# Where the operands of the MLP matmuls begin in SBUF: moving ones at a multiple of 64 bytes, stationary ones 32 past it

## The chip, the cores and the metric

The kernel runs on one core of one Trainium2 chip. The metric is device time of one execution in microseconds; three runs of the kernel before gave 1395.46, 1397.22 and 1397.25, median 1397.22.

## What is computed

Attention over 4 batches, 12 heads, 448 positions and 64 values a head, with the scores mixed across heads before the softmax and the weights mixed across heads after it. Its output, 1792 tokens of 768 values, goes through two MLPs one after the other; only the MLPs are touched here.

```python
def _moe_ref(x, w_in, w_out):              # first MLP
    h = x @ w_in                           # 1792x768 @ 768x2048
    g = np.where(h > 0.0, h, np.exp(np.minimum(h, 0.0)) - 1.0)
    return (g @ w_out).astype(np.float32)  # 1792x2048 @ 2048x768

def _moe2_ref(x, w_in, w_out):             # second MLP
    h = x @ w_in
    r = np.maximum(h, 0.0)
    return ((r * r) @ w_out).astype(np.float32)

x = np.ascontiguousarray(attn_out.transpose(0, 2, 1, 3)).reshape(B * S, H * D)
x = _moe_ref(x=x, **moe_kwargs)
return _moe2_ref(x=x, **moe2_kwargs)
```

## The kernel before

The attention runs first, and loads of the first weights and of x begin in its last steps. Then `Mlps.run` takes the 1792 tokens in two halves of 896. A half passes four stages: m = 0 is the first MLP, with its in-layer (x to h) and its out-layer (h to a new x), m = 1 the second, with its in-layer (x to h) and its out-layer (h to the output). Eight stages in all.

Every float32 operand is kept as two float32r tiles, a high part and the rest (`xh` and `xl`, `hh` and `hl`, `wh` and `wl`), and a product is three matmuls, written by `three` (L576 to L578): high by high, high by low, low by high, into one PSUM bank. A matmul streams its moving operand past a stationary one, which a weight load (PEld in the profile) put there while the matmul before it ran; here every matmul has a weight load of its own.

- In-layers (`inner`): stationary is a 128x128 block of a weight tile, moving are 448 columns of x. 16 blocks of h by 6 blocks of the contraction by 2 token blocks by 3 parts are 576 matmuls.
- Out-layer of the first MLP (in `run`): stationary is a block of a weight tile, moving are 448 columns of h. 6 by 16 by 2 by 3 are again 576.
- Out-layer of the second MLP: the roles are exchanged, so that the output comes with tokens on partitions. Stationary are 128 columns of h, moving are 384 columns of a weight tile. 2 by 16 by 7 by 3 are 672.

The order of the instructions is written out by hand in the loops, and each engine takes its own in that order. Weights are loaded by SyncE's queue, brought to float32 and split by ScalarE and VectorE (`Weights`, `part` last); `advance` keeps each of these steps a fixed number of units ahead of the matmuls. x and h are written by ScalarE (high part) and VectorE (rest).

Where an operand begins in its partition follows from where its tile was put and from the offset in it. All offsets inside x, h and the weights are multiples of 64 bytes (448 columns are 1792 bytes, 128 columns 512), so the start of the tile decides alone. In the kernel before, `xh`, `xl` and all buffers of `wh` and `wl` begin 32 bytes past a multiple of 64; `hh` and `hl` begin at a multiple of 64.

Of the kernel before, what the change touches and what calls it, by code (L numbers as in the profile page):

```python
# [8 lines left out]
F32R = mybir.dt.float32r  # L9
# [6 lines left out]
B, H, S, D = 4, 12, 448, 64  # L16
# [4 lines left out]
JC, NJ = 4, 112  # L21
KC, FC = DM // 128, DFF // 128
WU = 512
EXP_MIN, EXP_MAX = 2.0**-15, float.fromhex("0x1.dffffep+16")


# [367 lines left out]
class Weights:  # L394
# [6 lines left out]
    def __init__(self, nc, dram, layers):  # L401
        self.nc = nc
        self.units = []
        kept = [dram.tile([count, 128, n], F32, name=f"{name}f", tag=f"{name}f") for name, _, count, n in layers]
        for half in range(2):
            for k, (name, src, count, n) in zip(kept, layers):
                self.units += [(half, src[i], k[i], n) for i in range(count)]
        self.raw, self.single, self.parts, self.keep = {}, {}, {}, []
        self.loaded = self.sized = self.turned = self.done = self.used = 0

    def load(self, room=None):
        i = self.loaded
        self.loaded += 1
        half, src, kept, n = self.units[i]
        if half == 0:
            self.raw[i] = (room() if room else self.pool.tile([128, WU, 2], I32, name="wd", bufs=4))[:, :n, :]
            self.nc.sync.dma_start(out=self.raw[i].rearrange("p n t -> p (n t)"), in_=src.bitcast(I32))
        else:
            self.single[i] = self.pool.tile([128, WU], F32, name="wf", bufs=6)[:, :n]
            self.nc.sync.dma_start(out=self.single[i], in_=kept)  # L420

    def size(self, room=None):

        i = self.sized
        self.sized += 1
        half, src, kept, n = self.units[i]
        if half == 1:
            return
        f = (room() if room else self.pool.tile([128, WU], F32, name="wf", bufs=6))[:, :n]
        self.nc.scalar.activation(f, self.raw[i][:, :, 1].bitcast(F32), AF.Abs)  # L430
        self.single[i] = f
# [5 lines left out]
    def turn_op(self, k):  # L437

        nc = self.nc
        i = self.turned  # L440
        half, src, kept, n = self.units[i]
        if half == 0:
            if self.sized == i:
                self.size()
            t, f = self.raw[i], self.single[i]
            low, high, w = t[:, :, 0], t[:, :, 1], f.bitcast(I32)
            if k == 0:
                nc.vector.tensor_scalar(f, f, EXP_MIN, EXP_MAX, ALU.max, ALU.min)
            elif k == 1:
                nc.vector.tensor_scalar(w, w, 5, 2, ALU.logical_shift_left, ALU.logical_shift_right)  # L450
            elif k == 2:
                nc.vector.scalar_tensor_tensor(w, high, -0x40000000, w, ALU.bitwise_and, ALU.bitwise_or)
            else:
                nc.vector.scalar_tensor_tensor(w, low, 29, w, ALU.logical_shift_right, ALU.bitwise_or)  # L454
                del self.raw[i]
                self.keep.append((kept, f))
        self.turned += k == 3

    def part(self, engine=None):
        nc = self.nc  # L460
        i = self.done
        self.done += 1
        f = self.single.pop(i)
        n = self.units[i][3]
        hi = self.pool.tile([128, WU], F32R, name="wh", bufs=4)[:, :n]
        lo = self.pool.tile([128, WU], F32R, name="wl", bufs=4)[:, :n]
        nc.scalar.copy(hi, f)  # L467
        (engine or nc.vector).tensor_tensor(lo, f, hi.bitcast(F32), ALU.subtract)  # L468
        self.parts[i] = hi, lo
# [27 lines left out]
def col(i):  # L497
    return slice(i * 128, (i + 1) * 128)


class Mlps:
# [14 lines left out]
    def tmp(self):  # L516
        return self.tp.tile([128, S], F32, name="tmp", bufs=5)

    def two_parts(self, shape, pool, name):
        return [pool.tile(shape, F32R, name=f"{name}{a}", tag=f"{name}{a}") for a in "hl"]  # L520


    def plan(self, put, M, last, work, early, early_ctx, score_ctx):
# [29 lines left out]

    def new_x(self, half):
        self.half, self.xraw = half, {}
        self.nx = self.two_parts([128, KC, 2 * S], self.xp, "x")

    def piece(self, i):

# [37 lines left out]
    def run(self):  # L597
        nc, weights, blocks = self.nc, self.weights, self.blocks
        self.hp = self.pool("hp", "left")
        for half in range(2):  # L600
            xh, xl = self.nx
            for m in range(2):
                hh, hl = self.two_parts([128, FC, 2 * S], self.hp, "h")
                pending = []

                def activate(p, f, bl, m=m, hh=hh, hl=hl):
                    u = g = self.tmp()
                    if m == 0:
                        nc.scalar.activation(u, p, AF.Relu, scale=-1.0)
                        nc.scalar.activation(u, u, AF.Exp, scale=-1.0)  # L610
                        nc.vector.scalar_tensor_tensor(g, u, -1.0, p, ALU.add, ALU.max)
                    else:
                        nc.scalar.activation(u, p, AF.Relu)  # L613
                        nc.vector.tensor_tensor(g, u, u, ALU.mult)  # L614

                    def rest():
                        nc.scalar.copy(hh[:, f, bl], g)
                        nc.vector.tensor_tensor(hl[:, f, bl], g, hh[:, f, bl].bitcast(F32), ALU.subtract)

                    pending.append(rest)  # L620

                def flush():
                    for rest in pending:
                        rest()
                    pending.clear()

                for f in range(FC):
                    if half == m == f == 0:
                        p = self.begun
                    else:  # L630
                        p = self.inner(xh, xl, flush)
                    for j, bl in enumerate(blocks):
                        activate(p[j], f, bl)
                flush()
                if m == 0:
                    xh, xl = self.two_parts([128, KC, 2 * S], self.xp, "x")
                    for o in range(KC):
                        p = [self.bank()[:, :S] for _ in blocks]
                        for f4 in range(4):
                            wh, wl = weights.next()  # L640
                            for j, bl in enumerate(blocks):
                                for i in range(4):
                                    f = 4 * f4 + i
                                    self.three(p[j], wh[:, col(i)], wl[:, col(i)], hh[:, f, bl], hl[:, f, bl],
                                               f == 0, f == FC - 1)
                        for j, bl in enumerate(blocks):
                            nc.scalar.copy(xh[:, o, bl], p[j])
                            nc.vector.tensor_tensor(xl[:, o, bl], p[j], xh[:, o, bl].bitcast(F32), ALU.subtract)
                    continue
                n2 = DM // 2  # L650
                for nh in range(2):
                    p = [self.bank()[:, :n2] for _ in range(7)]
                    for f in range(FC):
                        if half == 0 and nh == 0:
                            if f == 0:
                                self.new_x(1)
                            if f < 12:
                                self.load_x(f)
                            if 2 <= f < 14:
                                self.split_x(f - 2)  # L660
                        wh, wl = weights.next()
                        for i in range(7):
                            self.three(p[i], hh[:, f, col(i)], hl[:, f, col(i)], wh[:, :n2], wl[:, :n2],
                                       f == 0, f == FC - 1)
                    for i in range(7):
                        o = self.tmp()[:, :n2]
                        if i % 2:
                            nc.scalar.copy(o, p[i])
                        else:
                            nc.vector.tensor_copy(o, p[i])  # L670
                        r = half * 2 * S + i * 128
                        nc.sync.dma_start(out=self.out[r : r + 128, nh * n2 : (nh + 1) * n2], in_=o)
# [49 lines left out]
```

## Time and profile before

| | before |
|---|---|
| three runs, median | 1397.22 us |
| the profiled execution, its own time | 1395.56 us |
| its span | 1393.8 us |
| TensorE matmuls busy | 1381.4 us, 99% |
| weight loads busy | 1249.7 us, 90% |
| VectorE, ScalarE, GpSimd busy | 62%, 48%, 19% |
| granted TensorE clock | 1.00 of 2.4 GHz |

Busy time of matmuls is no measure of how densely they follow each other: each is shown with 0.34 to 0.37 us, and the next begins 0.18 to 0.21 us after it. So the step from the start of one matmul to the start of the next is what to read, in the timeline, or as the length of a stage over its number of matmuls.

### The profile page before, as it was taken

Reading aid. Unit: us, or ns where it says so; the run is one execution under the profiler, and the core shown is the slowest. Engines: PE = TensorE matmul, PEld = TensorE weight load, DVE = VectorE, ACT = ScalarE, POOL = GpSimd, SP = SyncE. Lnnn points to the kernel's source line nnn. Section 1 sums busy time; section 2 is a strip of 40 time slices with the busy share of each in tenths; the row PEclk is TensorE's granted clock in tenths of the full one; section 3 lists DMA queues with packets and bytes.
Section 4 is the critical chain, followed back from the end, with each engine's and each line's share of the span. In section 5 each row is a group of like instructions: output and inputs, shape, how many; then the busy total and the mean of one; then the engine's idle time right before and its main releaser. Section 6 shows DMA issues by size and latency. Waiting matters only on the chain.

```text
span 1393.8 us, 24193 instructions
## 1 busy us (share of the span) xinstructions
PE 1381.4 (99%) x8906; PEld 1249.7 (90%) x8906; DVE 859.0 (62%) x1928; ACT 669.6 (48%) x1504; POOL 263.4 (19%) x245
## 2 busy tenths in 40 slices
PE   7999999999999999999999999999999999999999
PEld 4888888888889999999999999999999999999998
DVE  6877778777886989766688886534442114443121
ACT  5776767676775666322354543245541113333111
POOL 3755665665554000000000000000000000000000
PEclk9999999999999999999999999999999999999999
DMA  5624633734544555544455575431221111111131
GB/s 157 198 105 146 192 106 131 205 107 130 192 137 158 180 159 177 189 148 144 143 163 154 166 253 186 150 100 54 61 68 53 46 46 46 57 56 57 36 108 40
DMA packets 104810, 174.40 MB, mean 125 GB/s; under 512 B 22675, under 2 KB 82163, under 8 KB 104691
## 3 DMA queue, kind: packets, MB, share of 16 engines
q1 hardware_dynamic: 104691, 172.85, 39.4%
q8 instruction: 70, 1.15, 0.3%
q14 instruction: 49, 0.40, 0.1%
HBM read 97.93 MB, written 36.18 MB: 96 GB/s over the span
## 4 chain that ended last, share of the span: by engine, by line
PE 98%; DVE 1%; ACT 0%; DMA 0%; issue 0%; POOL 0%; SPq 0%; DVEq 0%
PE ps_post L220 12%; PE ps_qk L576 11%; PE ps_qk L577 11%; PE ps_qk L578 11%; PE ps_mix L577 6%; PE ps_post L577 6%; PE ps_mix L576 6%; PE ps_post L576 6%; PE ps_post L578 6%; PE ps_mix L578 6%; PE ps_qk L245 6%; PE ps_qk L162 4%; PE ps_mix L191 3%; PE ps_mix L190 2%; PE ps_mix L189 2%; DMA k_room<-kr 0%
## 5 line engine op out<-in xcount | busy, mean ns | idle before, releaser
L467 ACT CAST wh<-wf 128x384 fp32r<-128x384 f32 (+1 forms) x240 | 126.6, 532 | 272.4 <-DVE wf L454 113.8
L468 DVE TENSOR_TENSOR wl<-wf,wh 128x384 fp32r<-128x384 f32 (+1 forms) x238 | 137.3, 581 | 163.2 <-ACT wh L467 162.3
L183 POOL TENSOR_TENSOR gl<-graw,gh 120x448 fp32r<-120x448 f32 x178 | 201.5, 1154 | 145.7 <-ACT gh L178 142.4
L220 PEld LDWEIGHTS ps_post<-wg,ex 120*112 120x112 f32 x1440 | 156.1, 177 | 21.6 <-DVE tot L204 7.5
L220 PE MATMUL ps_post<-wg,ex 120*112 120x120 f32 x1440 | 172.9, 272 | 0.7 <-DVE at L227 0.6
L198 ACT ACTIVATE ex<-ps_mix,nmax 120x448 f32<-120x448 f32 x180 | 113.5, 637 | 113.5 <-DVE nmax L196 110.2
L576 PE MATMUL ps_qk<-xh,wh 128*128 128x448 f32 x384 | 141.4, 368 | 0.0
L577 PE MATMUL ps_qk<-xl,wh 128*128 128x448 f32 x384 | 141.3, 368 | 0.0
L578 PE MATMUL ps_qk<-xh,wl 128*128 128x448 f32 x384 | 141.3, 368 | 0.0
L196 DVE TENSOR_REDUCE nmax<-ps_mix 120x1 f32<-120x448 f32 x180 | 109.6, 622 | 41.7 <-PE ps_mix L191 41.3
L227 DVE COPY at<-ps_post 112x480 f32<-112x480 f32 x162 | 105.4, 650 | 9.9 <-PE ps_post L220 9.9
L178 ACT CAST gh<-graw 120x448 fp32r<-120x448 f32 x180 | 95.2, 593 | 0.1
L614 DVE TENSOR_TENSOR tmp<-tmp 128x448 f32<-128x448 f32 x64 | 39.9, 623 | 77.6 <-ACT tmp L613 77.6
L165 ACT COPY sc<-ps_qk 120x448 f32<-120x448 f32 x178 | 82.2, 558 | 7.1 <-PE ps_qk L162 7.0
L245 PEld LDWEIGHTS ps_qk<-at,v 112*64 112x64 f32 x1536 | 73.8, 137 | 11.3 <-ACT gh L178 6.5
L245 PE MATMUL ps_qk<-at,v 112*64 112x110 f32 (+2 forms) x1536 | 81.8, 262 | 0.0
L576 PEld LDWEIGHTS ps_qk<-xh,wh 128*128 128x128 f32 x384 | 72.1, 188 | 7.3
L577 PEld LDWEIGHTS ps_qk<-xl,wh 128*128 128x128 f32 x384 | 72.1, 188 | 7.3
L578 PEld LDWEIGHTS ps_qk<-xh,wl 128*128 128x128 f32 x384 | 72.1, 188 | 7.2
L430 ACT ACTIVATE wf<-wd 128x384 f32<-128x384 f32 (+1 forms) x120 | 69.4, 578 | 18.0 <-DMA wd<-w2o 8.6
L577 PE MATMUL ps_qk<-wl,hh 128*128 128x384 f32 x224 | 75.9, 339 | 0.0
L576 PE MATMUL ps_qk<-wh,hh 128*128 128x384 f32 x224 | 75.8, 339 | 0.0
(137 smaller groups left out, 3155.4 us busy)
## 6 DMA issues: line engine op xcount, KB each, us to landing
graw<-sc SPq DMA_DIRECT2D x180, 210.0 KB
wd<-w1i SPq DMA_DIRECT2D x32, 384.0 KB
wd<-w1o SPq DMA_DIRECT2D x24, 512.0 KB
wd<-w2i SPq DMA_DIRECT2D x32, 384.0 KB
wd<-w2o SPq DMA_DIRECT2D x32, 384.0 KB
w1if<-wf SPq DMA_DIRECT2D x32, 192.0 KB
w1of<-wf SPq DMA_DIRECT2D x24, 256.0 KB
w2if<-wf SPq DMA_DIRECT2D x32, 192.0 KB
```

Source lines behind the costliest of these rows:

```text
L178: nc.scalar.copy(hi, graw[t])
L183: engine.tensor_tensor(lo, graw.pop(t), parts[t][0].bitcast(F32), ALU.subtract)
L196: nc.vector.tensor_reduce(nmax, p, AX.X, ALU.max, negate=True)
L198: nc.scalar.activation(e[-1], p, AF.Exp, bias=nmax, scale=1.0, accum_out=tot[:, t % 2 : t % 2 + 1])
L220: nc.tensor.matmul(p[:, c, :], e[:, c * NJ : (c + 1) * NJ], w, start=True, stop=True)
L227: nc.vector.tensor_copy(o, p)
L245: nc.tensor.matmul(p[64 * a : 64 * a + 64, k, :w], vt[b, i][:, jc, g * D : (g + 1) * D], at[n][:, jc, 6 * i + g, :w], start=(jc == 0), sto ...
L467: nc.scalar.copy(hi, f)
L468: (engine or nc.vector).tensor_tensor(lo, f, hi.bitcast(F32), ALU.subtract)
L576: mm(p, wh, xh, start=first, stop=False)
L577: mm(p, wh, xl, start=False, stop=False)
L578: mm(p, wl, xh, start=False, stop=last)
```

## The change

A constant `OFF` of 8 elements, 32 bytes, is added. Tiles of x and h are made 64 bytes longer, and the operand begins in them `at` elements in: 8 for x, 0 for the h of the first MLP, 8 for the h of the second. The weight tiles keep their size; of the second out-layer's weights (`w2o`) the parts begin 8 elements into theirs, all others at 0. The tiles themselves also move a little, because x is longer: x by 128 bytes, the weight tiles by 128 bytes, `hl` by 64. With that the operands begin, in bytes past a multiple of 64:

| stage (of each half) | matmuls | moving, stationary before | moving, stationary after |
|---|---|---|---|
| first in-layer | 576 of 448 columns | x 32, w 32 | x 0, w 32 |
| first out-layer | 576 of 448 columns | h 0, w 32 | h 0, w 32 |
| second in-layer | 576 of 448 columns | x 32, w 32 | x 0, w 32 |
| second out-layer | 672 of 384 columns | w 32, h 0 | w 0, h 32 |

No engine gets an instruction more or less, and their order is the same on each. One load of x at the end of the attention no longer waits for TensorE, since the place that its tile has now was given up earlier.

```diff
+OFF = 8
@@ class Weights
-                self.units += [(half, src[i], k[i], n) for i in range(count)]
+                self.units += [(half, src[i], k[i], n, name == "w2o") for i in range(count)]
...
-        hi = self.pool.tile([128, WU], F32R, name="wh", bufs=4)[:, :n]
-        lo = self.pool.tile([128, WU], F32R, name="wl", bufs=4)[:, :n]
+        at = OFF * self.units[i][4]
+        hi = self.pool.tile([128, WU], F32R, name="wh", bufs=4)[:, at : at + n]
+        lo = self.pool.tile([128, WU], F32R, name="wl", bufs=4)[:, at : at + n]
@@ class Mlps
-    def two_parts(self, shape, pool, name):
-        return [pool.tile(shape, F32R, name=f"{name}{a}", tag=f"{name}{a}") for a in "hl"]
+    def two_parts(self, k, pool, name, at):
+        n = k * 2 * S
+        t = [pool.tile([128, n + 2 * OFF], F32R, name=f"{name}{a}", tag=f"{name}{a}") for a in "hl"]
+        return [x[:, at : at + n].rearrange("p (k s) -> p k s", k=k) for x in t]
...
-        self.nx = self.two_parts([128, KC, 2 * S], self.xp, "x")
+        self.nx = self.two_parts(KC, self.xp, "x", OFF)
...
-                hh, hl = self.two_parts([128, FC, 2 * S], self.hp, "h")
+                hh, hl = self.two_parts(FC, self.hp, "h", m * OFF)
...
-                    xh, xl = self.two_parts([128, KC, 2 * S], self.xp, "x")
+                    xh, xl = self.two_parts(KC, self.xp, "x", OFF)
```

## Rows read from the trace of the kernel before

**Rows 1.** The page: the span, busy time by engine, TensorE's granted clock, the chain.

```profile
span 1393.8 us, 24193 instructions
PE 1381.4 (99%) x8906; PEld 1249.7 (90%) x8906; DVE 859.0 (62%) x1928; ACT 669.6 (48%) x1504; POOL 263.4 (19%) x245
...
PEclk9999999999999999999999999999999999999999
...
PE 98%; DVE 1%; ACT 0%; DMA 0%; issue 0%; POOL 0%; SPq 0%; DVEq 0%
```

**Rows 2.** The windows of the eight stages: length, TensorE busy (matmuls touched), clock.

```profile
433.82:557.59 123.77, 123.77 (x675) 1.00 0.55 175
557.59:676.63 119.04, 119.04 (x578) 1.00 0.49 160
676.63:795.65 119.02, 119.02 (x577) 1.00 0.50 157
795.65:914.38 118.73, 118.73 (x674) 1.00 0.57 184
914.38:1033.41 119.03, 119.03 (x578) 1.00 0.24 72
1033.41:1152.44 119.03, 119.03 (x577) 1.00 0.17 49
1152.44:1271.47 119.03, 119.03 (x577) 1.00 0.19 54
1271.47:1393.80 122.33, 118.88 (x673) 1.00 0.20 62
```

**Rows 3.** Timeline of TensorE, first in-layer of half 1: start us, duration us.

```profile
999.72 0.37 PE L578 MATMUL ps_post<-xh,wl 128*128 128x448 f32 x1
999.93 0.37 PE L576 MATMUL ps_mix<-xh,wh 128*128 128x448 f32 x1
1000.14 0.37 PE L577 MATMUL ps_mix<-xl,wh 128*128 128x448 f32 x1
```

**Rows 4.** Timeline of TensorE in the first out-layer of half 0.

```profile
599.75 0.37 PE L576 MATMUL ps_post<-hh,wh 128*128 128x448 f32 x1
599.95 0.37 PE L577 MATMUL ps_post<-hl,wh 128*128 128x448 f32 x1
```

**Rows 5.** Timeline of TensorE in the second out-layer of half 0.

```profile
849.71 0.34 PE L576 MATMUL ps_mix<-wh,hh 128*128 128x384 f32 x1
849.89 0.34 PE L577 MATMUL ps_mix<-wl,hh 128*128 128x384 f32 x1
850.06 0.34 PE L578 MATMUL ps_mix<-wh,hl 128*128 128x384 f32 x1
850.24 0.34 PE L576 MATMUL ps_post<-wh,hh 128*128 128x384 f32 x1
```

**Rows 6.** Timeline of TensorE: the second and the 35th matmul of the first in-layer, and what follows.

```profile
434.11 0.36 PE L577 MATMUL ps_mix<-xl,wh 128*128 128x448 f32 x1
...
440.80 0.36 PE L577 MATMUL ps_post<-xl,wh 128*128 128x448 f32 x1
...
441.30 2.81 PE L245 MATMUL ps_qk<-at,v 112*64 112x108 f32 x56
```

**Rows 7.** Window between those two starts: length, busy, matmuls touched.

```profile
434.11:440.80 6.69, 6.69 (x35) 1.00 0.24 71
```

**Rows 8.** Timeline of TensorE in the attention: matmuls of 448 columns.

```profile
109.65 0.36 PE L189 MATMUL ps_mix<-gh,pre_l 120*120 120x448 f32 x1
109.85 0.36 PE L190 MATMUL ps_mix<-gh,pre_h 120*120 120x448 f32 x1
110.05 0.37 PE L191 MATMUL ps_mix<-gl,pre_h 120*120 120x448 f32 x1
```

**Rows 9.** The groups: weight loads of 128 and of 120 columns, mean ns.

```profile
L576 PEld LDWEIGHTS ps_qk<-xh,wh 128*128 128x128 f32 x384 | 72.1, 188 | 7.3
L190 PEld LDWEIGHTS ps_mix<-gh,pre_h 120*120 120x120 f32 x180 | 32.9, 183 | 1.8
```

More of the change, by code (lines that the diff above doesn't have):

```diff
@@ L413, in load @@
         self.loaded += 1
-        half, src, kept, n = self.units[i]
+        half, src, kept, n, moves = self.units[i]
         if half == 0:
@@ L425, in size @@
         self.sized += 1
-        half, src, kept, n = self.units[i]
+        half, src, kept, n, moves = self.units[i]
         if half == 1:
@@ L440, in turn_op @@
         i = self.turned
-        half, src, kept, n = self.units[i]
+        half, src, kept, n, moves = self.units[i]
         if half == 0:
```

## The prediction

> **What bounds the kernel now.** I read the page first: TensorE is busy for 99% of the span, 98% of the chain that ended last lies on it, and its clock was granted in full, 2.4 GHz, in every slice [rows 1]. So the kernel ends when TensorE has worked off its list, and no other engine's time matters unless it makes TensorE wait. Busy time does not say how dense the list is, so I read the stages next. The window of a stage goes from the start of its first matmul to the start of the next stage's first; the counts beside the windows are one or two above the stage's own, for the matmuls that straddle an end [rows 2]. A stage of 576 matmuls of 448 columns takes 119.03 us, which is 206.7 ns from start to start: both out-layers of the first MLP, the second in-layer of either half and the first in-layer of the second half, all alike within 0.02 us. The very first in-layer takes 123.77 us for as many, since the attention's last matmuls lie within it. The second out-layer, 672 matmuls of 384 columns, takes 118.73 us, 176.7 ns each; its second run, with the end of the program behind it in its window, has 118.88 us of busy time. Inside a stage the starts follow each other evenly, 0.20 to 0.21 us apart in an in-layer [rows 3] and in a first out-layer [rows 4], 0.17 to 0.18 in a second out-layer [rows 5], and no row of them names anything waited for.
>
> At 2.4 GHz, 448 clocks are 186.7 ns and 384 are 160.0. If a column takes a clock, a matmul carries 20.0 ns on top of its columns in the in-layers and the first out-layers, and 16.7 ns in the second out-layers. Those extras are all that a change of addresses could reach: 3456 x 20.0 + 1344 x 16.7 = 69 + 22 = 91 us, of 1395.56 us for the profiled execution (1393.8 span, 1.76 around it).
>
> **The change, part by part.** Nothing is added, removed or moved on any engine's list; SyncE's, GpSimd's and the other queues are as they were. One load of x loses a wait on TensorE at the end of the attention, where TensorE is the engine that others wait for: 0. ScalarE, VectorE and GpSimd write x, h and the last weights 32 bytes further on; they are busy 48%, 62% and 19% [rows 1] and TensorE waits for none of them in these stages, so even some per cent more on their writes stays under the matmuls: 0. What is left is how TensorE reads its two operands, stage by stage.
>
> First out-layers, 1152 matmuls: moving 0 and stationary 32 before and after. The tiles shift by multiples of 64 bytes. I take 0.
>
> In-layers, 2304 matmuls: from moving 32, stationary 32 to moving 0, stationary 32. The trace has this very case: it is the first out-layer, the same 448 columns against the same weight tiles, and it takes 119.04 and 119.03 us where the in-layers beside it take 119.02 and 119.03 [rows 2]. Moving 0 with stationary 32 and moving 32 with stationary 32 cost the same 206.7 ns. By that row the change here is 0, within 576 x 4 x 0.02 ns, under 0.1 us. It is the nearest row there can be, and I take it.
>
> But the spacing is not fixed by the addresses alone. The first 36 matmuls of the first in-layer use the same x and weight tiles as the rest of that stage, and from the second to the 35th the starts go from 434.11 to 440.80 [rows 6], 33 steps in 6.69 us [rows 7]: 202.7 ns, 4.0 less than later at the same alignment. So there are at least two steady rhythms at 32 and 32. In the attention, matmuls of 448 columns follow each other after 200 ns [rows 8], with loads of 120 columns in place of 128, 183 ns in place of 188 [rows 9]. That gives the in-layers' bounds: downward 2304 x 4.0 = 9.2 us by the first rhythm, 2304 x 6.7 = 15.4 us by the attention's; upward nothing shows more than 206.7 in a steady stretch, so 0.
>
> Second out-layers, 1344 matmuls: from moving 32, stationary 0 to moving 0, stationary 32, with 384 columns. No row has 384 columns in this arrangement. Two rows are near. The same stage with the alignments exchanged has 16.7 ns over its columns; the first out-layer, with the new alignments but 448 columns, has 20.0. If the columns' number or the mere chain of load and matmul sets the extra, it stays at 176.7 ns: 0. If the alignment sets it, it becomes 160.0 + 20.0 = 180.0: 1344 x 3.3 = 4.5 us more. Downward, the attention's rows leave 13.3 ns over the columns, 3.4 less than now: 4.5 us off. I take 0, because the in-layers and first out-layers show that 32 bytes in the start of the moving operand make no difference there, and the first 36 matmuls show that the extra differs where no alignment does. The sum is 0 + 0 + 0.
>
> The Trainium skill has a rule that speaks against the change (TensorE: Matmul & The Clock Gate, section Step-by-step: what each phase is for): TensorE reads the moving operand and the weights by two independent SBUF ports, and loading the next weights takes no read bandwidth from the running matmul. By it the sum is 0 as well. Its formula for isolated matmuls (section Back-to-back issue gap) would however give 448 / 2.4 + 2.5 = 189.2 ns, an estimate that the stages' 206.7 does not bear out; something costs 17.5 ns a matmul that the page does not name, so its rule is not proof that the two reads never meet.
>
> **The rivals.** *The exchange costs the second out-layers their shorter step.* Mechanism: the weight load and the running matmul meet in SBUF, and how often is set by where each begins. For it: all steady stretches with the stationary operand at 32 have 20.0 ns over the columns, all with it at 0 have 16.7 [rows 2]. Against it: 384 columns and stationary 0 always come together in this trace, and the first 36 matmuls have 16.0 with stationary 32. It decides if the extra belongs to the alignment; then 1397.2 + 4.5 = 1401.7 us, slower by 0.32%.
>
> *The in-layers fall into the shorter rhythm.* The stretch of 202.7 ns ended when the attention's matmuls cut in after the 36th [rows 6], and from then on all stages held 206.7. A new alignment could keep the shorter one: 2304 x 4.0 = 9.2 us, 1388.0 us; with the first out-layers too 3456 x 4.0 = 13.8, 1383.4; with the attention's 200 ns in the in-layers alone 15.4, 1381.8. For it: two rhythms exist at one alignment, so small things choose between them. Against it: the first out-layers have had the new alignment all along, and were at 206.7 in both halves.
>
> *The two reads stop meeting and the extra goes nearly whole.* The sum by rows is bounded by the 46 us that 20.0 ns on 2304 in-layer matmuls are, 1351 us. The first out-layers speak against it plainly, since they would have had it before. The page's 189.2 ns would make it 2304 x 17.5 = 40 us, 1357 us.
>
> That the change does not do what it says I leave at 0: the starts of the tiles after it are at the places that it names.
>
> **How the numbers follow.** Cases: all stages as they are 0.36 (1397.2 us); second out-layers slower 0.27 (1401.7); in-layers in a shorter rhythm 0.27 (1382 to 1393, the upper end with the second out-layers slower at the same time); second out-layers shorter alone 0.05 (1392.7); the extra gone 0.04; slower by something that no row shows 0.01. A measurement of this kernel can tell about 0.2%, 2.8 us, from no change: the three runs lie 1.8 us apart. Faster by more: 0.27 + 0.05 + 0.04 = 0.36. Within: 0.36. Slower: 0.27 + 0.01 = 0.28. The likeliest is no change, 1397.2 us; its own range is 1394.5 to 1400. Since both signs hold most of the chance together, the range for 8 in 10 goes from 1382, the attention's rhythm in the in-layers, to 1403, the slower second out-layers with a microsecond of the runs' spread; beyond it lie about 0.06.
>
> **What would show it.** Right: windows of 119.0 us for each stage of 576 and 118.7 for the second out-layers, TensorE's starts still 206.7 and 176.7 ns apart. The first rival shows as 121.0 us for each second out-layer with all else equal; the second as in-layers at 116.8 us or less (and first out-layers at 119.0 or at 116.8); the third as in-layers near 109. Wrong altogether I would be if the first out-layers moved much, since their alignments are the same before and after, or if a stage's starts became uneven, with a wait named between them.

## The result, and the profile after

The changed kernel takes 1381.26 us (median of 4 runs, 1381.01 to 1382.14) against 1396.43 us of the kernel before: a ratio of 0.9893, 95% interval 0.988 to 0.9905. That is 15.2 us, 1.1%, faster, where I had forecast no change; it lies 0.7 us below the range that I gave. Of 20 executions of the kernel before, 18 took 1395.4 to 1398.0 us and two, of which there is no profile, 1380.77 and 1378.98; both of these stand beside e11 below, and its interval is wide for that.

The page of the changed kernel, its span, busy times and TensorE's granted clock, to be set beside [rows 1]:

```profile
span 1379.2 us, 24193 instructions
PE 1368.4 (99%) x8906; PEld 1248.4 (91%) x8906; DVE 859.2 (62%) x1928; ACT 669.5 (49%) x1504; POOL 263.3 (19%) x245
...
PEclk9999999999999999999999999999999999999999
```

The same instructions, the other engines' busy times unchanged to some tenths of a us, TensorE's shorter by 13 us. The windows of its eight stages, in the order and with the columns of [rows 2] (stretch, length, TensorE busy, matmuls touched, clock):

```profile
434.94:556.94 122.00, 122.00 (x675) 1.00 0.55 177
556.94:674.06 117.12, 117.12 (x577) 1.00 0.50 164
674.06:791.18 117.12, 117.12 (x577) 1.00 0.50 159
791.18:907.68 116.50, 116.50 (x673) 1.00 0.59 188
907.68:1024.80 117.12, 117.12 (x577) 1.00 0.24 73
1024.80:1141.92 117.12, 117.12 (x577) 1.00 0.17 50
1141.92:1259.04 117.12, 117.12 (x577) 1.00 0.19 55
1259.04:1379.20 120.16, 116.66 (x673) 1.00 0.19 63
```

Every stage is shorter. A stage of 576 went from 119.03 to 117.12 us, 206.7 to 203.3 ns from start to start; a second out-layer from 118.73 to 116.50, 176.7 to 173.4 ns. The differences against [rows 2], in order, are 1.77, 1.92, 1.90, 2.23, 1.91, 1.91, 1.91 and 2.22 us: 15.8 together. The MLPs begin 1.1 us later in this execution, in a stretch of mean granted clock 0.99 where the execution before had 1.00; so the spans differ by 14.6 us.

The row to stop at is the second. It is the first out-layer, whose operands begin at 0 and at 32 past a multiple of 64 before and after. By the rule in the change's name nothing happened to it, and it gained as much as the in-layers. The starts in the second in-layer of half 0 (start us, duration us), to be set beside [rows 3]:

```profile
699.68 0.36 PE L581 MATMUL ps_qk<-xh,wh 128*128 128x448 f32 x1
699.89 0.37 PE L582 MATMUL ps_qk<-xl,wh 128*128 128x448 f32 x1
700.09 0.37 PE L583 MATMUL ps_qk<-xh,wl 128*128 128x448 f32 x1
700.29 0.36 PE L581 MATMUL ps_qk<-xh,wh 128*128 128x448 f32 x1
```

Hundredths of a us hide how even the steps are. By the starts in the trace, in ns, the steps here repeat 205, 200, 205, 205, 202, 204, each to within 1 ns or 2, where those of [rows 3] are all 206 or 207.

### The profile page after: what moved, and what is told of

Same layout as the page of the kernel before. It is cut to its first block, busy times and chain, and to the rows that moved or that the text cites. A ratio compares the mean times of both kernels' runs of the same rounds, so it can differ in the third digit from the quotient of the medians.

```text
span 1379.2 us, 24193 instructions
## 1 busy us (share of the span) xinstructions
PE 1368.4 (99%) x8906; PEld 1248.4 (91%) x8906; DVE 859.2 (62%) x1928; ACT 669.5 (49%) x1504; POOL 263.3 (19%) x245
## 4 chain that ended last, share of the span: by engine, by line
PE 97%; DVE 1%; ACT 0%; issue 0%; DMA 0%; POOL 0%; SPq 0%; ACTq 0%; DVEq 0%; POOLq 0%
PE ps_post L221 12%; PE ps_qk L582 11%; PE ps_qk L583 11%; PE ps_qk L581 11%; PE ps_qk L246 6%; PE ps_mix L582 6%; PE ps_post L582 6%; PE ps_post L583 6%; PE ps_mix L583 6%; PE ps_mix L581 6%; PE ps_post L581 6%; PE ps_qk L163 4%; PE ps_mix L192 3%; PE ps_mix L190 3%; PE ps_mix L191 3%
```

## The experiments

What the change did besides its rule: the tiles of x and h became 64 bytes longer, so that `xl` and `hl` now begin 64 bytes further on, modulo 128, than `xh` and `hh`; and the weight tiles moved by 128 bytes. So I put every operand's place in its own hands. In the kernel used for most runs, tiles of x and h are 256 bytes longer than before, which leaves all of them where they were modulo 256, and a table gives each operand's start modulo 256, by stage and half:

```diff
+PAD = 64
+PLACES = {'x1': (224, 224), 'x2': (224, 224), 'h1': (128, 128), 'h2': (128, 128),
+          'w1i': (224, 224), 'w1o': (224, 224), 'w2i': (224, 224), 'w2o': (224, 224)}
+BASE = {"x": 224, "h": 128, "w": 224}
+
+def at(kind, half, part):
+    name = kind[0]
+    place = PLACES.get((kind, half), PLACES[kind])[part]
+    return (place - BASE[name]) % 256 // 4
...
+        t = [pool.tile([128, n + PAD], F32R, name=f"{name}{a}", tag=f"{name}{a}") for a in "hl"]
+        o = [at(kind, half, a) for a in range(2)]
+        return [x[:, a : a + n].rearrange("p (k s) -> p k s", k=k) for x, a in zip(t, o)]
```

The table shown is the kernel before; with these places alone the longer tiles were not run, but stages at old places or old differences are among the runs below (e4, e6, e7). A pair is the high and the low part; x1, x2, h1, h2 are x and h of the first and second MLP, w1i to w2o the four weights. The changed kernel is x 128 and 192, h1 128 and 192, h2 160 and 224, all weights 96, but w2o 128.

### Same places modulo 64, both parts together (e1_together, e8_together_again)

```diff
-PLACES = {'x1': (224, 224), 'x2': (224, 224), 'h1': (128, 128), 'h2': (128, 128),
-          'w1i': (224, 224), 'w1o': (224, 224), 'w2i': (224, 224), 'w2o': (224, 224)}
+PLACES = {'x1': (128, 128), 'x2': (128, 128), 'h1': (128, 128), 'h2': (160, 160),
+          'w1i': (96, 96), 'w1o': (224, 224), 'w2i': (96, 96), 'w2o': (128, 128)}
```

> The changed kernel shortened every stage, the first out-layers too, whose operands begin at 0 and 32 past a multiple of 64 before and after; what changed there is that hl now begins 64 bytes past hh, counted by 128. This run keeps the change's places modulo 64 in all stages (in-layers and second out-layers moving 0, stationary 32) but puts the low part of x and of h at the same place modulo 128 as the high part. Theory of 64 bytes: what counts is the start modulo 64; in-layers 117.1 us and second out-layers 116.5 us as in the changed kernel, about 1384 us in all (first out-layers as before, 119.0). Theory of the parts apart: what counts is that the two moving parts begin 64 bytes apart, so that consecutive matmuls do not start at the same place of 128 bytes; in-layers and first out-layers 119.0 us again, second out-layers unknown, about 1393 to 1396 us. Theory of the rhythm: 206.7 ns is one rhythm that any shift of places can break, with no rule of addresses; the stages then come out unevenly, some at 119.0 and some at 117.1 or below, at the same alignment.

It took 1382.61 us, ratio 0.9905 (0.989 to 0.992). That would have passed for the theory of 64 bytes, had I looked at the time alone. The windows of its stages:

```profile
434.02:557.90 123.88, 123.88 (x676) 1.00 0.53 175
557.90:676.93 119.03, 119.03 (x578) 1.00 0.49 160
676.93:792.13 115.20, 115.20 (x577) 1.00 0.50 162
792.13:908.62 116.49, 116.49 (x674) 1.00 0.58 188
908.62:1026.37 117.75, 117.75 (x577) 1.00 0.24 72
1026.37:1141.58 115.21, 115.21 (x578) 1.00 0.17 51
1141.58:1260.60 119.02, 119.02 (x577) 1.00 0.19 54
```

The four in-layers have one and the same arrangement here and take 123.88 (with the attention's last matmuls in it, as before), 115.20, 117.75 and 119.02 us; the two first out-layers have one arrangement and take 119.03 and 115.21. So there is a step of 200.0 ns, shorter than any of the changed kernel's, and 206.7 at the same addresses, each held through a whole stage. The theory of 64 bytes falls, and so does that of the parts apart, by which in-layers and first out-layers would all be at 119.0. The second run of it:

> The run with the parts together a second time, to see whether the step that a stage falls into is the same in another execution. Theory of the rhythm: if the choice hangs on how the stage is entered, by things that vary between executions, the stages at 200.0, 204.4 and 206.7 ns are others than in the first run of it; if the entry is the same each time, they are the same. Theory of addresses: no stage can differ from another of the same places, which the first run of it has already shown otherwise.

It took 1383.46 us, and its eight windows were the same as those above within 0.01 us, the short ones and the long ones. The choice is the same in both profiled executions of this program.

### The old places, low parts 64 bytes apart (e2_apart)

```diff
-PLACES = {'x1': (224, 224), 'x2': (224, 224), 'h1': (128, 128), 'h2': (128, 128),
+PLACES = {'x1': (224, 32), 'x2': (224, 32), 'h1': (128, 192), 'h2': (128, 192),
```

> The kernel before, all operands at their old places modulo 64, but the low part of x and of h 64 bytes further on, modulo 128, than the high part (x: high 96, low 32; h: high 0, low 64; weights at 96). Theory of 64 bytes: nothing changes, stages 119.0 and 118.7 us, 1396 us. Theory of the parts apart: in-layers and first out-layers 117.1 us, six stages by 1.9 us less, 1384 us or somewhat less with the second out-layers, whose stationary parts are apart too. Theory of the rhythm: any mixture.

1384.03 us, ratio 0.9915 (0.9898 to 0.9931). All operands are at their old places modulo 64, and all stages shrink:

```profile
556.21:673.97 117.76, 117.76 (x578) 1.00 0.48 162
673.97:791.30 117.33, 117.33 (x578) 1.00 0.49 159
...
909.27:1026.60 117.33, 117.33 (x578) 1.00 0.24 73
1026.60:1144.36 117.76, 117.76 (x578) 1.00 0.16 50
1144.36:1261.68 117.32, 117.32 (x577) 1.00 0.19 54
```

12.5 us of the change's 15.2 come without its rule. And unlike in e1 equal arrangements take equal times: three in-layers 117.33, 117.33 and 117.32, two first out-layers 117.76. In these stages no second step appears. The second out-layers, whose stationary parts are apart here, did still differ, 117.97 us and 116.64 of busy time.

### Two maps by stage (e3_map1, e4_map2)

Here single halves have places of their own, the others those of the changed kernel, with w1o at 224. First e3, then e4:

```diff
+    ('x1', 0): (128, 160), ('h1', 0): (128, 0), ('x2', 0): (128, 224), ('h2', 0): (128, 128), ('w2o', 0): (128, 128),
+    ('x1', 1): (160, 224), ('w1i', 1): (128, 128), ('h1', 1): (128, 144), ('x2', 1): (128, 192), ('w2i', 1): (128, 128),
+    ('h2', 1): (128, 192), ('w2o', 1): (224, 224),
...
+    ('h2', 0): (128, 128), ('w2o', 0): (224, 224), ('w1i', 0): (96, 32), ('x2', 0): (224, 224), ('w2i', 0): (96, 32),
+    ('h1', 0): (192, 128), ('x1', 1): (224, 224), ('w1i', 1): (128, 128), ('x2', 1): (128, 128), ('w2i', 1): (128, 128),
+    ('h1', 1): (0, 0), ('h2', 1): (160, 224), ('w2o', 1): (128, 192),
```

> A map by stages, otherwise the changed kernel; places modulo 256. Half 0: x of the first in-layer high 128, low 160 with weights at 96 (32 apart); h 128 and 0 with weights at 224 (128 apart); x of the second in-layer 128 and 224 with weights 96 (96 apart); second out-layer weights 128 moving, h 128 stationary (both at 0 modulo 64). Half 1: x 160 and 224 with weights 128 (moving 32, stationary 0, parts 64 apart); h 128 and 144 with weights 224 (16 apart); x 128 and 192 with weights 128 (both 0, 64 apart); second out-layer weights 224 moving, h 128 and 192 stationary (the old places modulo 64, stationary parts apart). Theory of 64 bytes: 117.1 only in half 0's first stage as far as the high part goes and in the first out-layers, 119.0 in both in-layers of half 1, 118.7 in the second out-layers. Theory of the parts apart: 117.1 where the parts are 64 (perhaps 32, 96, 16) apart modulo 128, so in both in-layers of half 1, and 119.0 in half 0's first out-layer, whose parts are 128 apart. Theory of the rhythm: no order in it.

> A second map by stages, otherwise the changed kernel; places modulo 256. Half 0: first in-layer as changed (x 128 and 192) with the weights' parts apart, 96 and 32; first out-layer with the order turned, h 192 and 128, weights 224; second in-layer x 224 and 224, weights 96 and 32 (moving together, stationary apart); second out-layer at the old places, weights 224 moving, h 128 stationary. Half 1: first in-layer x 224, weights 128 (moving 32, stationary 0, together); first out-layer h 0 and 0, weights 224; second in-layer x 128, weights 128 (both 0, together); second out-layer weights 128 and 192 moving, h 160 and 224 stationary (both apart). Theory of 64 bytes: 117.1 in the first in-layer and the first out-layers; 119.0 in the second in-layers and in half 1's first in-layer; 118.7 in half 0's second out-layer and 116.5 in half 1's. Theory of the parts apart: 117.1 in half 0's first in-layer and first out-layer, 119.0 in half 1's first three stages and, unless stationary parts count as well, in half 0's second in-layer; 118.7 in half 0's second out-layer. Theory of the rhythm: stages with parts together fall to 117 or lower without order.

1382.49 and 1388.53 us. Of the second map's windows, those of the second out-layer at its old places, and of half 1's in-layer with moving 32 and stationary 0, its first out-layer with both h at 0, and its in-layer with all at 0:

```profile
792.39:911.11 118.72, 118.72 (x673) 1.00 0.56 184
911.11:1029.39 118.28, 118.28 (x578) 1.00 0.24 72
1029.39:1148.42 119.03, 119.03 (x577) 1.00 0.16 49
1148.42:1265.15 116.73, 116.73 (x577) 1.00 0.19 55
```

The first of these undoes one part of the change, and the second out-layer is back at the 118.73 of [rows 2]; so its gain is its own addresses'. The last has moving and stationary both at 0 and is shorter than the changed kernel's in-layers. In the first map, x at 160 and 224 with weights at 128 (moving 32, stationary 0) took 117.14 us, the changed kernel's 117.12 with everything shifted by 32 bytes; and x at 128 and 192 with weights at 128 took 117.33, what e2 took with everything shifted by 96. What these pairs have in common is the difference of the starts, moving less stationary: 32 and 96 for the two parts in one pair, 0 and 64 in the other.

### An extra matmul in the kernel before, all addresses as they were (e5_kick_before)

```diff
+    kicks = 0
+
+    def kick(self, p, w, x):
+        n = 384 + 2 * (self.kicks * 7 % 16)
+        self.kicks += 1
+        self.nc.tensor.matmul(p[:, :n], w[:, col(0)], x[:, :n], start=True, stop=True)
...
             wh, wl = self.weights.next()
+            if k3 == 0:
+                self.kick(p[0], wh, xh[:, 0])
...
                             wh, wl = weights.next()
+                            if f4 == 0:
+                                self.kick(p[0], wh, hh[:, 0])
```

> The kernel before with every operand at its old place; only one matmul is added ahead of each block of 36 matmuls of the in-layers and of 96 of the first out-layers, 76 in all, of 384 to 414 columns in changing lengths, into a bank that the next matmul overwrites. Theory of addresses (64 bytes, or parts apart): each block keeps the 206.7 ns of its stage after the extra matmul; the six stages come out longer by the extra matmuls alone, 76 x 0.19 = 14 us, about 1411 us. Theory of the rhythm: at the same addresses the blocks settle at different steps, some at 200.0, some at 202 to 205, some at 206.7 ns; a mean near 203.5 would make the 3456 matmuls shorter by 11 us, about 1400 us.

1398.12 us: 76 matmuls more, 14 us of work, for 1.2 us over the 1396.92 of the kernel before beside it. The windows of the first out-layer's six blocks, each an extra matmul of 0.18 us and 96 others:

```profile
559.64:579.03 19.39, 19.39 (x99) 1.00 0.62 195
579.03:598.41 19.38, 19.38 (x99) 1.00 0.58 188
598.41:617.81 19.40, 19.40 (x99) 1.00 0.49 163
617.81:637.83 20.02, 20.02 (x99) 1.00 0.47 158
637.83:657.84 20.01, 20.01 (x99) 1.00 0.45 145
657.84:677.24 19.40, 19.40 (x98) 1.00 0.37 126
```

(19.39 - 0.18) / 96 is 200.1 ns, (20.02 - 0.18) / 96 is 206.7. At one and the same addresses the blocks take the one step or the other. In the in-layers, 64 blocks, the second halves of the blocks had a mean step of 202.5 to 202.9 or of 206.6 to 206.7 and nothing else. The length of the extra matmul does not decide it alone: 384 columns were followed by the short step in three in-layers and by 206.7 ns in the fourth, here in half 1's first and second in-layer, windows of 36 matmuls:

```profile
991.42:998.72 7.30, 7.30 (x38) 1.00 0.20 56
1183.62:1191.06 7.44, 7.44 (x38) 1.00 0.18 53
```

So the kernel before had two rhythms at its addresses in the in-layers and two in the first out-layers, and its stages sat in the long one of either.

### The same in other places (e6_kick_map1, e7_kick_map2)

The extra matmul of e5, and these places for e6 and then e7; the rest as in e3:

```diff
+    ('x1', 0): (128, 128), ('x2', 0): (128, 192), ('x1', 1): (144, 144), ('x2', 1): (176, 176),
+    ('h1', 0): (128, 128), ('h1', 1): (128, 192),
...
+    ('x1', 0): (128, 128), ('w1i', 0): (128, 128), ('x2', 0): (224, 224), ('w2i', 0): (128, 128),
+    ('x1', 1): (192, 192), ('x2', 1): (128, 128), ('w2i', 1): (96, 32), ('h1', 0): (160, 160), ('h1', 1): (144, 144),
```

> The same extra matmuls in the changed kernel, with places of x and h by stage, modulo 256 (weights at 96 modulo 128 throughout). Half 0: first in-layer x 128 and 128, first out-layer h 128 and 128, second in-layer x 128 and 192 (as changed). Half 1: first in-layer x 144 and 144, first out-layer h 128 and 192 (as changed), second in-layer x 176 and 176. Theory of the rhythm: with both parts at the same place the blocks of a stage settle at 200.0, at 206.7 or between, by the length of the extra matmul; with the parts 64 apart they settle at 203.3 in nearly all blocks, since neither locked rhythm fits both parts. Theory of addresses: one step for each stage, whatever the extra matmul.

> The same, with other places. Half 0: first in-layer x 128, weights 128 (both at 0 modulo 64); first out-layer h 160, weights 224 (both at 32); second in-layer x 224, weights 128 (moving 32, stationary 0). Half 1: first in-layer x 192, weights 96; first out-layer h 144, weights 224 (moving 16 modulo 64); second in-layer x 128 and 128, weights 96 and 32 (stationary parts apart). Theory of the rhythm: where all four operands lie alike modulo 128 from one matmul to the next, the blocks fall to 200.0 or 206.7 by the extra matmul's length; a place at which all of them fall to 200.0 would be the one to build a kernel on. Theory of 64 bytes: moving 0 and stationary 32 (first in-layer of half 1) is the shortest in all blocks.

1396.82 and 1398.51 us, extra matmuls included. The mean step of each block's second half, for stages with both parts together: x 128 with weights 96, 200.0, 204.4 and 206.7, by block; h 128 with weights 224, 200.0 and 206.7, by block, as in e5; x 128 with weights 128, 202.5 to 202.9 and 206.7, which are the two of e5's in-layers, where x and weights both lay at 224; x 224 with weights 128 and x 192 with weights 96, 205.1 to 205.5 in all blocks of both; h 160 with weights 224, 202.3 in all. The parts 64 apart, as in the changed kernel's in-layers: 203.2 to 203.3 in all 16 blocks. So the places do have a say: they fix which steps a stage can hold. And what counts of them is again the difference, 0 in one pair of stages, 96 in the other. The choice repeats too: the first in-layer with x and weights at 128 (e7) and at 224 (e5) took the same one of its two steps in all 16 blocks, and half 0's first out-layer did so in all 6 (e5, e6). That points to how a block is entered; what of the entry counts, beside the extra matmul, is not shown.

### The difference put to the test (e9_diff1, e10_diff2)

As e6, with these places (w1i and w2i at 96, w1o at 224); first e9, then e10:

```diff
+    ('x1', 0): (160, 160), ('x2', 0): (224, 224), ('x1', 1): (64, 64), ('x2', 1): (112, 112),
+    ('h1', 0): (80, 80), ('h1', 1): (112, 112), ('w2o', 0): (192, 192), ('w2o', 1): (0, 0),
...
+    ('x1', 0): (48, 48), ('x2', 0): (80, 80), ('x1', 1): (104, 104), ('x2', 1): (208, 208),
+    ('h1', 0): (96, 96), ('h1', 1): (192, 192), ('w2o', 0): (160, 160), ('w2o', 1): (64, 64),
```

In both h2 lies at 128 in either half.

> The runs so far put to order by the difference of the two starts, moving less stationary, modulo 256: 0 settles at 202.7 or 206.7 ns, 32 at 200.0, 204.4 or 206.7, 160 at 200.0 or 206.7, 48 at 202.9, 80 at 203.4, 96 at 205.4, 176 at 204.2, 192 at 202.3, wherever the two lie. Theory of the difference: it alone fixes which steps a stage can settle at, and the entry chooses among them. This run (extra matmuls as before, both parts at one place) tries 64, 128, 224 and 16 in the in-layers and 112 and 144 in the first out-layers, and in the second out-layers 64 and 128. By the theory each stage has one step or a small set of them between 200 and 207 ns, 173 to 177 in the second out-layers; and 128, 224 and 112 come out here and in the next run, at other absolute places, with the same set. Theory of the rhythm alone (no rule of addresses): the same differences come out unlike in the two runs.

> The same with differences 208, 240, 8 and 112 in the in-layers and 128 and 224 in the first out-layers, 32 and 192 in the second out-layers. Theory of the difference: 112, 128 and 224 have the same steps as in the run before, where x and h had them the other way round. A difference whose only step is 200.0 ns or less would be the one to build on. Theory of the rhythm alone: no agreement between the two runs.

1398.36 and 1400.96 us, extra matmuls included. Three differences were set up twice, once in x and once in h, at other absolute places. 112 gave 206.7 ns in all 6 blocks of h and 206.6 to 206.7 in all 16 of x. 128 gave 203.5 to 204.4 in 16 blocks of x and 203.8 to 204.1 in 6 of h. 224 gave 203.3 to 204.6 in x and in h. Settled blocks of each, as windows of 96 matmuls in h and 36 in x: for 112 one of h in e9 and one of x in e10, for 128 one of h in e10 and one of x in e9, for 224 two of h in e10 and two of x in e9:

```profile
598.05:617.90 19.85, 19.85 (x98) 1.00 0.48 159
1171.77:1179.21 7.44, 7.44 (x37) 1.00 0.19 55
...
598.81:618.38 19.57, 19.57 (x97) 1.00 0.51 161
708.21:715.55 7.34, 7.34 (x37) 1.00 0.47 161
...
1057.72:1077.24 19.52, 19.52 (x97) 1.00 0.20 55
1097.23:1116.86 19.63, 19.63 (x97) 1.00 0.18 53
952.63:959.96 7.33, 7.33 (x38) 1.00 0.18 54
975.21:982.57 7.36, 7.36 (x38) 1.00 0.20 55
```

That is 206.8 and 206.7 ns a matmul for 112, 203.9 twice for 128, and 203.3 to 203.6 or 204.4 to 204.5 for 224. The expectation that the difference alone fixes the set was borne out three times, and the difference of 64 had a mean step of 199.9 to 200.2 in all 16 blocks.

### A version built on the difference of 64 (e11_diff64), and its neighbours (e12_near64)

```diff
-PLACES = {'x1': (224, 224), 'x2': (224, 224), 'h1': (128, 128), 'h2': (128, 128),
+PLACES = {'x1': (32, 32), 'x2': (32, 32), 'h1': (32, 32), 'h2': (160, 160),
```

> No extra matmuls. The weights at their places of the kernel before (224 modulo 256), x and h both parts at 32, so that moving less stationary is 64 in the in-layers and first out-layers, and in the second out-layers h at 160, weights at 224, again 64. Moving and stationary operands so begin alike modulo 64 (all at 32), which the change's rule forbids. Theory of the difference: at 64 the in-layers' only step was 200.0 ns and the second out-layers' 173.3; the six stages of 576 come to 115.2 us, the second out-layers to 116.5, the first stage some 4 to 5 us above the others, and the kernel to 1396.5 less 3456 x 6.67 less 1344 x 3.33, about 1369 us, some 12 us below the changed kernel. Theory of 64 bytes: all stages as bad as or worse than in the kernel before, 1396 us or more.

1368.67 us (four runs, 1368.22 to 1369.17): 12.6 us below the changed kernel, 27.2 below the 1395.86 of the seven runs of the kernel before beside it. The ratio stands at 0.9823 with a wide interval, 0.9751 to 0.9894; the shortest of those seven is still 9.8 us above the longest of these four. Its windows, without the first stage and the last:

```profile
553.78:668.98 115.20, 115.20 (x578) 1.00 0.50 166
668.98:784.18 115.20, 115.20 (x577) 1.00 0.52 161
784.18:900.67 116.49, 116.49 (x674) 1.00 0.59 188
900.67:1015.88 115.21, 115.21 (x577) 1.00 0.25 74
1015.88:1131.08 115.20, 115.20 (x577) 1.00 0.18 51
1131.08:1246.29 115.21, 115.21 (x578) 1.00 0.19 55
```

Each as forecast to 0.01 or 0.02 us, with moving and stationary operands at the same 32 bytes past a multiple of 64, which is what the change set out to avoid.

The neighbours, as e9 with these places:

```diff
+    ('x1', 0): (152, 152), ('x2', 0): (168, 168), ('x1', 1): (164, 164), ('x2', 1): (160, 32),
+    ('h1', 0): (32, 32), ('h1', 1): (32, 224), ('w2o', 0): (184, 184), ('w2o', 1): (144, 144),
```

> Extra matmuls as before, to see how sharp the difference of 64 is and whether another is shorter. In-layers: 56 and 72 (half 0, first and second), 68 and parts at 64 and 192 (half 1); first out-layers: 64 together, then parts at 64 and 0; second out-layers 56 and 16. Theory of the difference: 64 in the first out-layer gives 200.0 ns in all blocks, as it did in an in-layer; the neighbours may lie a few ns off, and parts at different differences settle between. If none is below 200.0, the version with 64 is the shortest of those tried.

1398.17 us, extra matmuls included. At 64 the first out-layer had 200.0 ns in all six blocks. Four bytes further, at 68, all 16 blocks had 206.2 to 207.1; at 72, 206.2 to 207.8; at 56, 200.4, 204.5 or 205.0 by block. Parts at 64 and 192 gave 199.9 or 204.5, parts at 64 and 0 gave 202.2. Nothing was below the 200.0 of 64 by more than the 0.1 ns that the cut of the blocks leaves open. All differences tried with both parts together, for 448 columns:

| moving less stationary, modulo 256 | mean step of the blocks, ns |
|---|---|
| 0 (before: in-layers) | 202.7 or 206.7 |
| 8, 68, 72 | 206.2 to 207.8 |
| 16 | 202.0 to 202.5, twice 200.0 |
| 32 | 200.0, 204.4 or 206.7 |
| 48; 80; 96 | 202.8 to 203.2; 203.4, once 206.6; 205.4 |
| 56 | 200.4, 204.5 or 205.0 |
| 64 | 200.0 |
| 112; 144 | 206.7; 206.7 |
| 128; 208 | 203.5 to 204.4; 203.8 to 204.2 |
| 160 (before: first out-layers) | 200.0 or 206.7 |
| 176; 192; 240 | 204.2; 202.3; 202.7 |
| 224 | 203.3 or 204.4 |

For the second out-layers, 384 columns: 176.7 ns at 96 (the kernel before) and at 32, 173.3 to 173.4 at 0, 64 and 224, and 174.7 to 176.0 at 16, 56, 128 and 192.

## Why the prediction was wrong

**What bounds the kernel: right.** TensorE's list is the bound, and the shorter steps went into the end: 15.8 us in the eight windows, 14.6 in the span, since the MLPs began 1.1 us later. The reserve was where I put it, in the step beyond the columns. That the starts follow each other evenly was right for the steps of 206.7; in the second out-layers the rows' hundredths hid a cycle of 178, 174, 180, 175 ns.

**First out-layers, "I take 0": wrong, 1.91 us each.** This step failed first. I held the change to its name and counted the places modulo 64. The table behind e12 shows that what counts is moving less stationary, and modulo 256 at least: 0 and 128 hold other steps, and so do 32 and 160, 64 and 192. Before it was 160 for both parts, with 200.0 and 206.7 to choose from; after it is 32 for `hh` and 96 for `hl`, which holds 203.3. The shift by multiples of 64 that I waved through is all that changed for these stages' operands.

**In-layers, "the nearest row there can be": wrong, 1.9 us each.** The row was the first out-layer, alike modulo 64, and it was not alike in what counts: 160 against 32 and 96. That it took the same 119.03 us as the in-layers was a coincidence of two sets, {202.7, 206.7} at a difference of 0 and {200.0, 206.7} at 160, which share their long step. The evidence for a second step was in the rows: the first 36 matmuls at 202.7 ns [rows 6, 7] and the attention's 200 [rows 8]. I read the former rightly, as a second rhythm at the same addresses, and gave it its price, but then let the equal windows decide. e5 shows that rhythm in more than half of the in-layers' blocks at the old addresses.

**Second out-layers, 0 with a rival of 4.5 us more: wrong in both.** They became shorter by 2.2 us each, 4.5 us together. The rival's mechanism, that the alignment sets the step, is nearer to what the runs show than my reason for 0, but its sign was taken from the first out-layer's row, again by places modulo 64. With the old addresses put back in e4 the stage is at 118.72 us again; four other arrangements reach 116.5. The bound that I drew from the attention's rows, 4.5 us off, is what came; that the size fits is luck, since those matmuls have other loads and no run ties the two together.

**The rivals.** The one that came is "the in-layers fall into a shorter rhythm". Its version with the first out-layers gave 1383.4 us, 2.1 from the time measured, and that is partly luck: the second out-layers' 4.5 us were missing from it, and 203.3 ns is not the 202.7 that I priced it with. The stages did not keep a rhythm that they had; at other differences they took one that was not open to them before. 4800 x 3.3 is 15.8 us, which is what the windows give. I had given all of it 0.27, and cut the range at 1382 because I let the terms go down one at a time. With the second out-layers' own lower bound in the same case the range would have reached 1377 and held the time. "The extra goes nearly whole" came in none of the arrangements tried: the shortest step is 200.0 ns, 13.3 over the columns. "Wrong altogether I would be if the first out-layers moved much" was the right thing to look at.

**The two ports: no guide to the sum.** With equal instructions the step goes from 200.0 to 206.7 ns by where the two operands begin against each other. The Trainium skill, TensorE: Matmul & The Clock Gate (section Step-by-step: what each phase is for), has loading the next weights take no SBUF read bandwidth from the running matmul. That rule gives no reason for such a dependence, and the sum of 0 that goes with it did not come; but no run here shows the two reads taking anything from each other either.

## What to carry to other kernels

Where float32r matmuls of 384 or 448 columns, as here, follow each other with a weight load each, read the step from start to start, not the busy time, and treat the start of the moving operand less that of the stationary one as a parameter to be scanned; a stage's window divided by its matmuls shows the answer to 0.1 ns, even from a single profile. A comparison of times cannot tell a rule of alignment from a change of rhythm: look whether stages with equal arrangement take equal times before believing either. And an edit that lengthens a tile moves every tile put after it, so compare all addresses, not only those that the edit names.

## What was not expected of the hardware

A stage settles, mostly within some tens of matmuls, in a rhythm that it holds to its end, such as 200.0, 202.7, 203.3, 204.4 or 206.7 ns. Which of them are open to it is fixed, as far as tried, by moving less stationary, and at several differences there are two or three, between which a single extra matmul ahead of a block can decide (e5, e6), though not by its length alone. At 64 and at 112 there was no choice: 22 blocks of 22 at 200.0, and 22 of 22 at 206.7 (206.6 in some). How sharp that is was a surprise: 64 gives 200.0, 68 gives 206.5.

A mean can stand for a cycle. By the starts in the traces, in ns, the 202.7 of [rows 7] is 199, 207, 202, 203, 202 over and over, five steps where the program's parts come round every three; e11's in-layers repeat 201, 201, 198. The stages at 206.7 of the kernel before and e1's second in-layer at 200.0 keep one step to within 1 ns. The weight loads do not show it in their recorded time: 188 ns in [rows 9], at steps of mostly 206.7, and the same in e11 at 200.0:

```profile
L597 PEld LDWEIGHTS ps_qk<-xh,wh 128*128 128x128 f32 x384 | 72.1, 188 | 5.8
```

What makes these rhythms is not settled. That the step depends on where the two reads stand against each other, and not on where either stands, fits two streams that meet in SBUF while a weight load runs beside a matmul; but no run here shows the meeting itself, the pattern of the differences has no order that I could find, and whether more than 256 bytes count was not tried. If all in-layers and first out-layers of the kernel before fell into the shorter of their two steps, it would take 2304 x 4.0 + 1152 x 6.7 = 16.9 us less, 1379.5 for 1396.4; no profile shows it so.
